# Attention and a token-mixing layer on one core: the same operations written in another order

## The chip, the cores and the metric

The kernel runs on one core of a Trainium2 chip. The metric is device microseconds of one execution, from start to end; less is better. The median of three runs of the kernel before is 121.55 us (121.43 to 121.94).

## The reference

Inputs are fp32; the output is fp32 of 8 x 576 x 512. For each of 8 batches and 8 heads, 32 packed queries `p` attend to 576 keys and values, and the 576 queries `q` then attend to the 32 packed results. The heads are joined to `x` of 576 x 512, and a layer without a softmax mixes the tokens:

```
p_packed = softmax(scale * p @ k.T) @ v              # 32 x 64 per head
out      = softmax(scale * q @ p_packed.T) @ p_packed  # 576 x 64 per head
x        = join_heads(out)                             # 576 x 512 per batch
W        = scale2 * (x @ w_q) @ (x @ w_k).T            # 576 x 576
result   = relu(W @ x) @ w_out
```

## The kernel before

The engines are TensorE (PE), VectorE (DVE), ScalarE (ACT), GpSimd (POOL) and SyncE (SP, which issues transfers). The kernel is a set of small named operations for a batch, each of one engine, and a string `SCHEDULE` (lines 10 to 62) that lists them in the order in which they are recorded. The loop at line 789 reads the string and calls each one. Each engine does its instructions in the order of the string; between engines semaphores hold an instruction until its inputs are there and until its buffer is free. So the string sets the order of each engine and, through it, of all work. No other rule plans it.

An item is `name@batch`, and behind it:

- for PE a colon, the PSUM banks (0 to 4) that it writes, and sometimes a letter: `c` writes the work as halves of 64 columns, `f` as 128 columns, `p` in both ways;
- for an eviction out of PSUM the engine that does it: `v` DVE, `s` ACT. `g` is POOL, and `p` behind a store is SP;
- nothing where only one engine does it.

```
    for item in SCHEDULE.split():
        name, rest = item.split("@")
```

The operations of a batch, in the order of their data:

- `LK`, `LQ`, `LV` load k, q and v (0.59 MB each as bf16) with a transfer that POOL issues and that turns fp32 into bf16 on the way. Batch 0 loads q and v in halves (`LQA`, `LVA`, `LQB`, `LVB`), and its k comes in fp32 through SP at the kernel's start and is cast by `cA0` to `cB1`. `cw` and `wo` load the layer's weights, `LP` loads p. Six buffers stand for each of k, q and v.
- `kt`, `qt` transpose k and q on PE (line 262) in three parts, `ke`, `qe` evict them. Batch 0 does this in four parts, `kf`/`kfe` and `qf`/`qfe`. `tp`, `lp` (batch 0) and `tr`, `lq0`, `lq1` (all others, four scalings each) prepare p's transpose.
- `s0` computes the first scores (line 321), `nm0` takes their maximum on DVE (line 335), `ex0`, `ex1` the exponential on ACT (line 344). `xt`/`xe` transpose the result and evict it, `rc1` takes the reciprocal of the sums, `pv` multiplies with v (line 423), `pp0`, `pp1` scale and mask on DVE, `pt`/`pte` transpose again.
- `e0` computes the second scores (line 507). Then `mx0` (maximum, line 523), `sb0` (subtraction, 526), `x0` (exponential on ACT, 533), `sm0` (sum, 537), `rr0` (reciprocal, 540), and three products on POOL, `ml0`, `ml1`, `ml2` (line 561). `at`/`ae` transpose and evict the product.
- `pq`, `wk`, `wkx`, `wq`, `g`, `y` are the layer's small matmuls, with evictions of the same name and an `e` behind; `m0`, `m1`, `m2` mix the tokens (lines 697 and 719), `r..` evict with the relu, `o0` to `o4` multiply with `w_out` (line 737), `oe..` evict, `st` and `sc` store. The last blocks are stored alone, `o2` of batch 7 in two halves (`o2a`, `o2b`).

Batch 0 is done in halves of its heads at many places (`sA`, `sB`, `nmA`, `pvA`, `ptA`, `mxA` and so on). The scores `s` and the second scores `e_ps` share one buffer of three PSUM banks, so `s0` of a batch waits for `sb0` of another and `e0` for `ex0` and `ex1`. All other PE results turn over in five banks.

`wm@n` (line 782) is PE work whose result nobody reads: n pairs of matmuls of 512 columns with the identity matrix. There are 22 pairs, 9 of them ahead of k's first transposes.

Of the kernel before, what the change touches and what calls it, by code (L numbers as in the profile page):

```python
# [7 lines left out]


SCHEDULE = """  # L10
    wm@8:4 LP@0 LQA@0 LVA@0 cA0@0s cA1@0v LQB@0 wm@1:4 pc@0v kf1@0:2 LVB@0 tp@0:0 kf0@0:4
# [29 lines left out]
    kt1@7:0 ke0@7s qt2@5:2 g@3:1f ke2@7s ke1@7v o3@2:4f sm0@4 ex1@6 pv@5:30 ex0@6 ge@3v
    rr0@4 qe2@5s s0@7 pp1@5 ml0@4g pp0@5 oe3@2s y@3:0 xt1@6:2f nm0@7 pt@5:1f xe1@6s ml2@4g
    xt0@6:4f at0@4:3f ml1@4g ye@3s o2@2:2f ae0@4v ex1@7 pte@5v at1@4:0f xe0@6v oe2@2s
    m2@3:1f ae1@4v qt0@6:4 ex0@7 rc1@6 st1@2 pq@4:3 qt2@6:0 qe0@6v qt0@7:2 pqe@4s st1@1
    qe2@6v e0@5:c r2@3s st0@2 qe0@7s wk@4:0f mx0@5 st0@1 xt0@7:4c wke@4s m1@3:23 o4@3:1f
    r11@3s wkx@4 r10@3s sb0@5 g@4:3f pv@6:02 ge@4s oe4@3s xe0@7v qt1@6:1 pp1@6 y@4:4 wq@4:3
    pp0@6 qe1@6s qt2@7:2 ye@4v xt1@7:0c x0@5 qe2@7v pt@6:4c o2@3:1f pte@6v xe1@7v wqe@4s
    sm0@5 o3@3:4f oe2@3s qt1@7:0 oe3@3s e0@6:p rr0@5 qe1@7v ml0@5g st1@3 m0@4:41 rc1@7 mx0@6
    pv@7:23 r01@4s ml2@5g r00@4s m0@3:10 ml1@5g pp1@7 o1@4:4c r01@3s pp0@7 r00@3s sb0@6
    pq@5:0 at0@5:2c pqe@5s at1@5:3c ae0@5s pt@7:1c o0@3:0c ae1@5v x0@6 pte@7v wk@5:2p  # L50
    o1@3:3c wkx@5 oe1@4s sm0@6 wke@5s m1@4:41 oe1@3s e0@7:p r11@4s wq@5:3 rr0@6 oe0@3s mx0@7
    g@5:2c ml0@6g r10@4s o0@4:1c st0@3 ge@5s wqe@5s st2@3 y@5:2 ml2@6g o3@4:0c sb0@7 ml1@6g
    ye@5s oe0@4s pq@6:2 at0@6:3c oe3@4s m2@5:4c pqe@6v st0@4 at1@6:1c x0@7 ae0@6v m0@5:20
    ae1@6v o2@4:3c r00@5v r2@5s sm0@7 wk@6:1p r01@5s o4@5:2c oe2@4s wq@6:0 wke@6v st1@4
    oe4@5s wkx@6 m1@5:43 rr0@7 g@6:1c st2@5 r10@5s r11@5v o0@5:2c ml2@7g ge@6s wqe@6v ml1@7g
    o3@5:1c oe0@5v ml0@7g at1@7:0c y@6:4 pq@7:3 o2@5:2c ye@6s pqe@7v oe3@5s ae1@7v at0@7:4c
    m0@6:31 ae0@7s o1@5:0c r00@6v oe2@5s r01@6v wk@7:3p st1@5 oe1@5s m1@6:24 wkx@7 o0@6:1c
    r10@6v st0@5 wke@7s r11@6s g@7:3c oe0@6s o1@6:2c ge@7v y@7:3 wq@7:0 oe1@6s o2@6:1c ye@7s
# [770 lines left out]
```

## Time and profile before

| | us |
|---|---|
| median of three runs | 121.55 (121.43 to 121.94) |
| the profiled execution | 122.1 |
| its span in the profile | 120.3 |
| PE busy | 109.1 |
| DVE busy | 99.4 |
| ACT busy | 86.8 |
| POOL busy | 44.7 |

The profile is of one execution. Its page gives the busy time of each engine over the span, the same in forty slices of 3 us, the chain of work that ended last, and groups of instructions by line. Times are from the start of the span. A matmul's end is modelled, so PE's busy time holds short waits. The trace also gives instructions in order of time; counted along the schedule, they give each operation its start.

The loads are one stream: from 5.4 us to 83.9 us the queue that carries them has no gap longer than 0.3 us.

### The profile page before, as it was taken

The numbers are of one execution on the slowest core, as the hardware profiler recorded it, in microseconds if no ns is written. First come the engines' busy times: TensorE is split into PE (matmuls) and PEld (weight loads), VectorE is DVE, ScalarE is ACT, GpSimd is POOL, SyncE is SP. The second block draws the span as 40 slices with busy tenths as digits, with TensorE's granted clock in tenths as the row PEclk, the third lists the DMA queues.
The fourth block names the chain that finished last, engine by engine and source line by source line (L and its number), as shares of the span: only waits on it lengthen the run. The fifth ranks groups of instructions, "written<-read, shape, count | busy, mean of one in ns | idle before, by whom it ended". The sixth has DMA issues, their size and how long they took to land.

```text
span 120.3 us, 4812 instructions
## 1 busy us (share of the span) xinstructions
PE 109.1 (91%) x2121; PEld 76.5 (64%) x2121; DVE 99.4 (83%) x176; ACT 86.8 (72%) x169; POOL 44.7 (37%) x70
## 2 busy tenths in 40 slices
PE   5999786588999999999999999999999999999950
...
DVE  3278799968999979999999999989998999566330
...
GB/s 70 375 165 195 207 208 190 207 208 206 211 205 212 204 209 208 206 208 207 208 226 306 290 209 208 209 255 398 225 180 1 106 335 197 70 230 267 185 291 171
DMA packets 18165, 25.47 MB, mean 212 GB/s; under 512 B 2272, under 2 KB 14816, under 8 KB 18144
## 3 DMA queue, kind: packets, MB, share of 16 engines
...
## 4 chain that ended last, share of the span: by engine, by line
PE 70%; DVE 19%; POOL 2%; ACT 2%; issue 2%; POOLq 0%; DVEq 0%
PE o_ps L737 24%; PE tp_h L262 9%; PE warm L787 6%; PE pv L423 4%; PE m_ps L697 4%; PE tp_a L582 3%; DVE rs L537 3%; PE e_ps L507 3%; PE wq_ps L642 3%; PE tp_x L399 2%; POOL a L561 2%; PE s L321 2%; DVE e L526 2%; DVE mx L523 2%; PE wk_ps L619 2%
## 5 line engine op out<-in xcount | busy, mean ns | idle before, releaser
L561 POOL TENSOR_TENSOR a<-e,rr 128x512 bf16<-128x512 f32 (+1 forms) x24 | 19.3, 828 | 50.4 <-DVE rr L540 45.1
L737 PE MATMUL o_ps<-w_out,reluT 128*64 128x512 bf16 (+2 forms) x236 | 32.3, 373 | 0.1
L737 PEld LDWEIGHTS <-reluT 128*64 128x64 bf16 (+1 forms) x236 | 13.8, 108 | 9.6 <-issue 1.0
L143 ACT ACTIVATE o_sb<-o_ps 128x512 f32<-128x512 f32 x25 | 14.9, 602 | 3.7 <-PE o_ps L737 3.2
L143 ACT ACTIVATE kT<-tp_h 128x768 bf16<-128x768 bf16 (+2 forms) x13 | 9.8, 794 | 5.7 <-PE tp_h L262 5.6
L143 ACT ACTIVATE reluT<-m_ps 128x512 bf16<-128x512 f32 x20 | 11.5, 600 | 2.5 <-PE m_ps L697 2.2
L344 ACT ACTIVATE e1T<-s,nmax 128x576 bf16<-128x576 f32 x16 | 11.8, 755 | 0.6 <-DVE nmax L338 0.5
L262 PE MATMUL tp_h<-ident,q_sb 128*64 128x128 bf16 x288 | 11.9, 221 | 0.2 <-ACT pqk L143 0.2
L533 ACT ACTIVATE e<-e 128x1152 f32<-128x1152 f32 (+2 forms) x9 | 9.5, 1059 | 3.3 <-DVE e L526 3.3
L262 PEld LDWEIGHTS <-q_sb 128*64 128x64 bf16 x288 | 9.8, 110 | 2.8 <-issue 1.7
L523 DVE TENSOR_REDUCE mx<-e_ps 128x36 f32<-128x1152 f32 (+2 forms) x9 | 10.9, 1208 | 0.7 <-PE e_ps L507 0.4
L262 PE MATMUL tp_h<-ident,k_sb 128*64 128x128 bf16 x288 | 11.3, 226 | 0.0
L526 DVE TENSOR_TENSOR e<-e_ps,mx 128x1152 f32<-128x1152 f32 (+2 forms) x9 | 11.0, 1221 | 0.3
L537 DVE TENSOR_REDUCE rs<-e 128x36 f32<-128x1152 f32 (+2 forms) x9 | 10.9, 1211 | 0.2 <-ACT e L533 0.2
L262 PEld LDWEIGHTS <-k_sb 128*64 128x64 bf16 x288 | 9.7, 114 | 1.0 <-issue 0.2
L787 PE MATMUL warm<-ident 128*64 128x512 bf16 x44 | 8.4, 488 | 1.5 <-POOL ident masks.py:199 1.4
L335 DVE TENSOR_REDUCE nmax<-s 128x2 f32<-128x1152 f32 x7 | 9.3, 1327 | 0.0
L145 DVE TENSOR_SCALAR reluT<-m_ps 128x512 bf16<-128x512 f32 x12 | 8.1, 679 | 1.3 <-PE m_ps L697 1.3
L149 DVE COPY qT<-tp_h 128x768 bf16<-128x768 bf16 (+2 forms) x16 | 8.4, 533 | 0.8 <-PE tp_h L262 0.4
L423 PE MATMUL pv<-v_sb,e 64*128 64x256 bf16 x126 | 8.1, 270 | 0.0
L582 PE MATMUL tp_a<-ident,a 128*64 128x128 bf16 (+1 forms) x113 | 6.4, 221 | 1.7 <-POOL a L561 1.7
L143 ACT ACTIVATE qT<-tp_h 128x768 bf16<-128x768 bf16 (+1 forms) x9 | 7.1, 798 | 0.9 <-PE tp_h L262 0.7
...
## 6 DMA issues: line engine op xcount, KB each, us to landing
...
```

The lines of the kernel that those rows point to most:

```text
L143: nc.scalar.activation(dst, src, func, scale=scale)
L262: nc.tensor.transpose(dst[64 * g2:64 * g2 + 64], src[:, g2], ident)
L344: nc.scalar.activation(tile("e1T", [P, NJ, 2, 64], bf16, b)[:, :, h2], S_[b]["s1"][0][h2].rearrange("r (j s) -> r j s", j=NJ), EXP, bias=S ...
L423: nc.tensor.matmul(ps[h2], S_[b]["e1"][r, j, :], S_[b]["v_sb"][r, :, j, :].rearrange("s (g gp) d -> s gp g d", gp=2), start=(j == 0), stop ...
L523: nc.vector.tensor_reduce(tile("mx", [P, NU, 1], fp32, b)[:, r], S_[b]["e"][:, r], axis=AX, op=MAX)
L526: nc.vector.tensor_tensor(tile("e2", [P, NU, L], fp32, b)[:, r], S_[b]["e"][:, r], S_[b]["mx"][:, r].to_broadcast((P, nu, L)), op=SUB,)
L533: nc.scalar.activation(e, e, EXP, scale=scale)
L537: nc.vector.tensor_reduce(tile("rs", [P, NU, 1], fp32, b)[:, r], src[:, r], axis=AX, op=ADD)
L561: (nc.gpsimd if on == "g" else nc.vector).tensor_tensor(tile("a2", [P, NU, L], bf16, b)[:, r], S_[b]["e2"][:, r], S_[b]["rr"][:, r].to_bro ...
L582: nc.tensor.transpose(tp[r, k - k0], a2(b, k % 4 if k < 8 else 4, k // 4)[:, r], ident)
L737: nc.tensor.matmul(ps[r], src[:, i, o:o + P][:, r], w_out[:, i, cols], start=(i == 0), stop=(i == 3),)
L787: nc.tensor.matmul(ps[r], ident[:, r], moving, start=True, stop=True)
```

## The change

Only `SCHEDULE` changes. Every operation stays except the unread pairs, 23 instead of 22: `wm@2:2 wm@1:2 wm@10:4` at the head, so 13 stand ahead of k's first transposes (`kf1`, `kf0`) and 10 of them write one bank in a row. The other 10 stand later.

- 45 evictions and casts go from ACT to DVE and 43 from DVE to ACT; one store goes from SP to ACT and one back. The second part of k's cast (`cA0`) goes to DVE, behind `pc`; `lq1` goes to ACT, behind `ex1@0`; all relu evictions of `m0` and `m1` of batch 0 go to ACT.
- The letters of PE's operations change: 75 have the letter `c` instead of 61, 17 have `f` instead of 33, 11 have `p` instead of 9.
- The order of q's and v's loads at the head stays as it was, `LQA`, `LVA`, `LQB`, `LVB`. On POOL, `LK@3` goes ahead of `ml0@0`, `wo0` goes between `ml1@0` and `ml2@0`, `LQ@5` goes behind `ml1@2`, `LK@7` and `LV@5` go behind `ml0@3`, `LV@6` goes ahead of `LQ@7`, and `LV@7` goes behind `ml2@4`.
- DVE's order from `mx0` of batch 2 to that of batch 3 was mx0@2, ye@1, ke0@4, sb0@2, r01@1, pp0@3, pp1@3, nm0@4, qe0@3, sm0@2, qe1@3, pte@3, rr0@2, r11@1, ke0@6, mx0@3. It is now mx0@2, ke0@4, sb0@2, r00@1, pp1@3, pp0@3, nm0@4, qe2@3, qe0@3, qe1@3, sm0@2, rr0@2, mx0@3.
- The last PE operations were o1, o0, o2b, o2a of batch 7 and are now o2a, o0, o1, o2b. ACT ended with the evictions oe1, oe0 and the stores sc0, sc2b; it now ends with oe0, oe1, sc1, sc2b.

The diff, cut:

```diff
-    wm@8:4 LP@0 LQA@0 LVA@0 cA0@0s cA1@0v LQB@0 wm@1:4 pc@0v kf1@0:2 LVB@0 tp@0:0 kf0@0:4
-    lp@0v LK@1 wm@3:3 kfe0@0s kfe1@0v wm@2:3 cB1@0v LK@2 cB0@0v sA@0 wm@1:3 cw3@0 nmA@0
-    kf3@0:1 kf2@0:3 kfe3@0s cw0@0 tr@0:42 kfe2@0v ex0@0 wm@2:3 lq1@0v lq0@0s sB@0 cw2@0
-    wm@1:3 xa0@0:3 nmB@0 xa1@0:0 xea0@0s qf0@0:2 rcA@0 xea1@0v ex1@0 qf1@0:1 cw1@0 qfe0@0v
-    pvA@0:0 qfe1@0s xb0@0:4 pp0@0 xb1@0:2 xeb0@0s LQ@1 rcB@0 xeb1@0v ptA@0:1f qf3@0:3
-    pteA@0s qfe3@0v e0A@0 wm@4:1 mxA@0 sbA@0 pvB@0:0 LV@1 qf2@0:2 xA@0 pp1@0 qfe2@0v
-    ptB@0:4c smA@0 pteB@0s e0B@0 rrA@0 mxB@0 ml0@0g kt2@1:3 kt1@1:1 sbB@0 ke2@1s kt0@1:0
-    LK@3 at0@0:4c ke0@1v xB@0 ke1@1v ae0@0s smB@0 s0@1 kt0@2:4 rrB@0 nm0@1 kt2@2:1 ml2@0g
-    kt1@2:0 ke2@2s ml1@0g pq@0:2 ke1@2v pqe@0s wo0@0 ex1@1 at1@0:1c ae1@0v wo1@0 ex0@1
-    ke0@2v wq@0:1 LQ@2 wk@0:2p wqe@0s LV@2 s0@2 wkx@0 qt0@1:4 wke@0s LK@4 nm0@2 xt0@1:3f
...
-    pt@1:0c xe0@2v pte@1s m1@0:23 xe1@2v e0@1:c r10@0s LK@6 rc1@2 r11@0v kt1@3:4 mx0@1
-    kt0@3:0 ke1@3s kt2@3:1 LK@5 ke2@3s pq@1:4 sb0@1 o1@0:3c pqe@1s LQ@4 o2@0:4c ke0@3v x0@1
-    oe1@0v s0@3 oe2@0s o0@0:3c sm0@1 qt0@2:4 oe0@0s qt1@2:0 rr0@1 qt2@2:1 qe1@2s nm0@3
-    o3@0:3c ml0@1g qe0@2s ml2@1g oe3@0v at0@1:2f ex1@3 ml1@1g pv@2:40 ae0@1v ex0@3 qe2@2v
-    LV@4 at1@1:2c pp0@2 xt0@3:1f ae1@1s pp1@2 LQ@5 xt1@3:3f rc1@3 xe0@3v pt@2:0c wk@1:2c
-    pte@2s e0@2:f wkx@1 LK@7 wke@1s kt0@4:4 xe1@3s mx0@2 g@1:1c wq@1:0 ge@1s y@1:2 wqe@1s
-    kt1@4:3 ye@1v kt2@4:1 ke0@4v ke1@4s pv@3:02 sb0@2 LV@5 ke2@4s m0@1:43 m2@1:1c r00@1s
-    r01@1v s0@4 x0@2 pp0@3 o0@1:3c pp1@3 nm0@4 r2@1s qt2@3:2 pq@2:0 qt0@3:4 qe2@3s o1@1:1c
-    qe0@3v pqe@2s sm0@2 oe0@1s o4@1:2c oe1@1s qt1@3:0 ex1@4 pt@3:3c qe1@3v kt2@6:1 ex0@4
-    pte@3v m1@1:40 rr0@2 kt0@6:3 r10@1s r11@1v e0@3:c ml1@2g ke2@6s ke0@6v o3@1:0f mx0@3
...
-    st2@1 qt0@4:4 xe1@4v s0@5 wkx@2 qe0@4s st0@0 sm0@3 wq@2:0 wke@2s kt1@6:2 st1@0 wqe@2s
-    qt2@4:4 pv@4:13 qe2@4s rr0@3 nm0@5 ml0@3g pq@3:4 g@2:0c pqe@3s LQ@7 pp1@4 ge@2s qt1@4:4
-    ex1@5 pp0@4 y@2:3 ml1@3g ke1@6v pt@4:1f ye@2s at0@3:0f qe1@4v pte@4s m0@2:32 ex0@5
...
-    mx0@4 at1@3:0f xt0@5:1f ae1@3s o1@2:2f xe1@5s sb0@4 qt0@5:0 xe0@5s wq@3:3 oe1@2s o0@2:1c
...
-    r00@7v r01@7s st1@6 o3@7:1c oe4@7s o1@7:2c st2@7 oe3@7v o0@7:0c oe1@7s sc3@7p o2b@7:3c
-    sc1@7p oe0@7s o2a@7:2c oe2b@7v sc0@7s oe2a@7v sc2b@7s sc2a@7p
+    wm@2:2 wm@1:2 wm@10:4 LP@0 LQA@0 LVA@0 cA1@0v LQB@0 pc@0v cA0@0v LVB@0 tp@0:2 LK@1
+    kf1@0:3 lp@0v kf0@0:4 kfe1@0s wm@3:0 LK@2 kfe0@0v cB1@0s cB0@0v sA@0 cw0@0 wm@2:1 nmA@0
+    kf3@0:3 kf2@0:0 kfe3@0v tr@0:24 ex0@0 cw2@0 kfe2@0v sB@0 lq0@0s wm@1:0 nmB@0 cw3@0
+    xa0@0:0 xa1@0:1 rcA@0 qf0@0:3 xea0@0s xea1@0v qf1@0:2 ex1@0 qfe0@0v pvA@0:1 cw1@0
+    qfe1@0v lq1@0s pp0@0 xb0@0:0 xb1@0:2 xeb0@0v ptA@0:1f xeb1@0v qf2@0:0 LQ@1 pteA@0v e0A@0
+    qfe2@0v wm@4:2 mxA@0 rcB@0 sbA@0 pvB@0:0 xA@0 LV@1 qf3@0:1 pp1@0 qfe3@0v ptB@0:0c smA@0
+    pteB@0s e0B@0 rrA@0 mxB@0 kt0@1:3 LK@3 kt1@1:4 sbB@0 ke0@1s kt2@1:1 ml0@0g ke1@1v xB@0
+    ke2@1v at0@0:4c smB@0 s0@1 ae0@0s kt1@2:2 rrB@0 nm0@1 kt2@2:0 ml1@0g kt0@2:4 ke2@2s
+    pq@0:1 wo0@0 ke0@2v ex1@1 ke1@2v ml2@0g ex0@1 wo1@0 at1@0:2c LQ@2 ae1@0v pqe@0s s0@2
...
+    y@0:0 xt0@2:1c pp1@1 ye@0s qe1@1v xe0@2s pt@1:2c xt1@2:4c rc1@2 pte@1v m1@0:30 xe1@2s
+    e0@1:c LK@6 r10@0s r11@0s m0@0:14 mx0@1 kt1@3:3 r00@0s LK@5 kt2@3:0 r01@0s kt0@3:2
+    ke1@3s sb0@1 o2@0:1c LQ@4 ke0@3s o1@0:3c ke2@3v x0@1 pq@1:4 o0@0:2c pqe@1s sm0@1 oe1@0s
+    s0@3 oe2@0s o3@0:3c oe0@0s rr0@1 nm0@3 qt0@2:4 ml0@1g oe3@0s qt2@2:1 qt1@2:2 qe0@2s
+    ml1@1g qe1@2v at0@1:0f ex1@3 pv@2:34 qe2@2v ae0@1v ex0@3 ml2@1g LV@4 at1@1:2f pp1@2
+    xt0@3:0f pp0@2 ae1@1s xt1@3:1f xe0@3v pt@2:4f xe1@3v wk@1:3p pte@2s rc1@3 kt2@4:0 wke@1v
+    e0@2:c wkx@1 ke2@4s g@1:3f mx0@2 wq@1:4 ge@1s y@1:2 kt0@4:3 wqe@1s kt1@4:1 ke0@4v ye@1s
+    sb0@2 ke1@4s m0@1:34 pv@3:02 r01@1s r00@1v x0@2 m2@1:4c s0@4 pp1@3 o0@1:3c pp0@3 r2@1s
+    nm0@4 pt@3:2c oe0@1s qt2@3:0 qt1@3:4 pte@3s qe2@3v qt0@3:3 ex1@4 o1@1:2c qe0@3v ex0@4
+    qe1@3v m1@1:10 sm0@2 oe1@1s kt0@6:4 e0@3:c ke0@6s o4@1:2f rr0@2 r10@1s mx0@3 ml1@2g
+    r11@1s pq@2:3 kt2@6:1 pqe@2s o3@1:4c ke2@6s LQ@5 sb0@3 xt0@4:3c ml0@2g oe3@1s kt0@5:0
...
+    wk@2:4p qe2@4s rr0@3 pv@4:23 wke@2v ex0@5 ml0@3g rc1@4 qe0@4v ex1@5 wkx@2 wq@2:1 pp1@4
+    LK@7 kt1@6:0 wqe@2s pp0@4 g@2:3c LV@5 ke1@6v at0@3:4c ge@2s pt@4:1c ae0@3v y@2:2 ml1@3g
...
+    r11@2v LQ@6 e0@4:p r00@2s r10@2v at1@3:4c LV@6 r01@2s xt0@5:1f mx0@4 ae1@3s qt0@5:3 LQ@7
...
+    pq@4:1 nm0@7 y@3:4 qe2@5s o2@2:2c ml2@4g LV@7 ye@3s at1@4:3f pqe@4v ex0@7 ml0@4g pt@5:0f
...
+    o1@3:2c sm0@6 wke@5s r11@4s g@5:1c e0@7:p ge@5s rr0@6 oe1@3s pq@6:0 r10@4v y@5:3 o0@4:1c
...
+    o3@6:4c r2@7s st0@6 m1@7:10 o4@7:3f r10@7s r11@7v oe3@6s m0@7:02 oe4@7v o3@7:4c st1@6
+    r00@7s r01@7v st2@7 o2a@7:3c oe3@7v o0@7:0c oe2a@7v sc3@7p o1@7:3c oe0@7s sc2a@7p
+    o2b@7:4c sc0@7p oe1@7s oe2b@7v sc1@7s sc2b@7s
```

More of the change, by code (lines that the diff above doesn't have):

```diff
@@ L17 @@
-    ptB@0:4c smA@0 pteB@0s e0B@0 rrA@0 mxB@0 ml0@0g kt2@1:3 kt1@1:1 sbB@0 ke2@1s kt0@1:0
-    LK@3 at0@0:4c ke0@1v xB@0 ke1@1v ae0@0s smB@0 s0@1 kt0@2:4 rrB@0 nm0@1 kt2@2:1 ml2@0g
-    kt1@2:0 ke2@2s ml1@0g pq@0:2 ke1@2v pqe@0s wo0@0 ex1@1 at1@0:1c ae1@0v wo1@0 ex0@1
-    ke0@2v wq@0:1 LQ@2 wk@0:2p wqe@0s LV@2 s0@2 wkx@0 qt0@1:4 wke@0s LK@4 nm0@2 xt0@1:3f
-    g@0:1f LV@3 qt1@1:0 ge@0s xe0@1s y@0:2 qe1@1v xt1@1:1c ye@0s rc1@1 xe1@1v ex0@2 m0@0:30
-    pv@1:21 r00@0v LQ@3 ex1@2 qe0@1v r01@0s qt2@1:3 pp1@1 xt0@2:4c pp0@1 xt1@2:1c qe2@1v
@@ L29 @@
-    kt1@4:3 ye@1v kt2@4:1 ke0@4v ke1@4s pv@3:02 sb0@2 LV@5 ke2@4s m0@1:43 m2@1:1c r00@1s
-    r01@1v s0@4 x0@2 pp0@3 o0@1:3c pp1@3 nm0@4 r2@1s qt2@3:2 pq@2:0 qt0@3:4 qe2@3s o1@1:1c
-    qe0@3v pqe@2s sm0@2 oe0@1s o4@1:2c oe1@1s qt1@3:0 ex1@4 pt@3:3c qe1@3v kt2@6:1 ex0@4
-    pte@3v m1@1:40 rr0@2 kt0@6:3 r10@1s r11@1v e0@3:c ml1@2g ke2@6s ke0@6v o3@1:0f mx0@3
-    ml2@2g ml0@2g xt0@4:3f oe3@1s kt1@5:4 xe0@4v kt2@5:0 LQ@6 ke1@5s sb0@3 at1@2:3f at0@2:1f
-    ke2@5s o2@1:4f ae1@2v ae0@2s xt1@4:0f rc1@4 oe4@1s oe2@1v kt0@5:3 x0@3 wk@2:1p ke0@5v
@@ L35 @@
-    st2@1 qt0@4:4 xe1@4v s0@5 wkx@2 qe0@4s st0@0 sm0@3 wq@2:0 wke@2s kt1@6:2 st1@0 wqe@2s
-    qt2@4:4 pv@4:13 qe2@4s rr0@3 nm0@5 ml0@3g pq@3:4 g@2:0c pqe@3s LQ@7 pp1@4 ge@2s qt1@4:4
-    ex1@5 pp0@4 y@2:3 ml1@3g ke1@6v pt@4:1f ye@2s at0@3:0f qe1@4v pte@4s m0@2:32 ex0@5
-    ae0@3v ml2@3g m1@2:14 r00@2v LV@6 qt1@5:0 r01@2s e0@4:p qe1@5v LV@7 r10@2s xt1@5:3f
-    mx0@4 at1@3:0f xt0@5:1f ae1@3s o1@2:2f xe1@5s sb0@4 qt0@5:0 xe0@5s wq@3:3 oe1@2s o0@2:1c
-    rc1@5 r11@2v wqe@3s qe0@5v wk@3:2p x0@4 s0@6 wkx@3 wke@3v kt0@7:4 oe0@2s nm0@6 kt2@7:3
@@ L41 @@
[L41 to L58, printed above, removed]
@@ L59 @@
-    wqe@7v st0@6 m2@7:4c oe2@6v m1@7:02 o3@6:3c r11@7s r2@7v r10@7s m0@7:42 oe3@6s o4@7:0c
-    r00@7v r01@7s st1@6 o3@7:1c oe4@7s o1@7:2c st2@7 oe3@7v o0@7:0c oe1@7s sc3@7p o2b@7:3c
-    sc1@7p oe0@7s o2a@7:2c oe2b@7v sc0@7s oe2a@7v sc2b@7s sc2a@7p
+    wm@2:2 wm@1:2 wm@10:4 LP@0 LQA@0 LVA@0 cA1@0v LQB@0 pc@0v cA0@0v LVB@0 tp@0:2 LK@1
+    kf1@0:3 lp@0v kf0@0:4 kfe1@0s wm@3:0 LK@2 kfe0@0v cB1@0s cB0@0v sA@0 cw0@0 wm@2:1 nmA@0
+    kf3@0:3 kf2@0:0 kfe3@0v tr@0:24 ex0@0 cw2@0 kfe2@0v sB@0 lq0@0s wm@1:0 nmB@0 cw3@0
@@ new lines @@
+    rc1@1 LV@2 xt1@1:3c nm0@2 wk@0:2p xt0@1:0c LK@4 qt0@1:4 xe0@1s qt2@1:1 LV@3 wkx@0 qe0@1s
+    wke@0v wq@0:0 xe1@1v ex0@2 qe2@1v g@0:3f ge@0v ex1@2 pv@1:42 wqe@0v LQ@3 qt1@1:3 pp0@1
+    y@0:0 xt0@2:1c pp1@1 ye@0s qe1@1v xe0@2s pt@1:2c xt1@2:4c rc1@2 pte@1v m1@0:30 xe1@2s
+    e0@1:c LK@6 r10@0s r11@0s m0@0:14 mx0@1 kt1@3:3 r00@0s LK@5 kt2@3:0 r01@0s kt0@3:2
+    ke1@3s sb0@1 o2@0:1c LQ@4 ke0@3s o1@0:3c ke2@3v x0@1 pq@1:4 o0@0:2c pqe@1s sm0@1 oe1@0s
+    s0@3 oe2@0s o3@0:3c oe0@0s rr0@1 nm0@3 qt0@2:4 ml0@1g oe3@0s qt2@2:1 qt1@2:2 qe0@2s
@@ new lines @@
+    r11@1s pq@2:3 kt2@6:1 pqe@2s o3@1:4c ke2@6s LQ@5 sb0@3 xt0@4:3c ml0@2g oe3@1s kt0@5:0
+    kt1@5:1 xe0@4v kt2@5:4 x0@3 ml2@2g ke1@5v o2@1:3f ke0@5v oe4@1s ke2@5v at1@2:1f xt1@4:0c
+    sm0@3 ae1@2s st2@1 at0@2:4c s0@5 xe1@4s qt2@4:1 ae0@2s st1@0 nm0@5 qt0@4:0 oe2@1s st0@0
+    wk@2:4p qe2@4s rr0@3 pv@4:23 wke@2v ex0@5 ml0@3g rc1@4 qe0@4v ex1@5 wkx@2 wq@2:1 pp1@4
+    LK@7 kt1@6:0 wqe@2s pp0@4 g@2:3c LV@5 ke1@6v at0@3:4c ge@2s pt@4:1c ae0@3v y@2:2 ml1@3g
+    qt1@4:0 pte@4s pq@3:3 ye@2s qt1@5:4 qe1@4v pqe@3s m1@2:21 qe1@5s rc1@5 ml2@3g m0@2:30
@@ new lines @@
+    r11@2v LQ@6 e0@4:p r00@2s r10@2v at1@3:4c LV@6 r01@2s xt0@5:1f mx0@4 ae1@3s qt0@5:3 LQ@7
+    o0@2:2c xe0@5s sb0@4 o1@2:1c oe0@2s qe0@5s xt1@5:0c wk@3:4p xe1@5v x0@4 s0@6 wkx@3
+    wke@3v kt1@7:2 nm0@6 oe1@2s wq@3:4 ke1@7s kt2@7:0 kt0@7:1 ke2@7v o3@2:3c ex1@6 ke0@7v
+    ex0@6 sm0@4 g@3:1f pv@5:02 ge@3s oe3@2s wqe@3s rr0@4 s0@7 pp0@5 ml1@4g pp1@5 qt2@5:3
+    pq@4:1 nm0@7 y@3:4 qe2@5s o2@2:2c ml2@4g LV@7 ye@3s at1@4:3f pqe@4v ex0@7 ml0@4g pt@5:0f
+    oe2@2v xt0@6:1f qt0@6:4 ex1@7 rc1@6 pte@5v st1@2 xt1@6:2c xe0@6v m2@3:0c xe1@6s st1@1
```

14 lines of the change are left out of this document (added).

## The prediction

> **What bounds the kernel now.** I read the page first, then the busy time in stretches, then the chain of waits, then the instructions in order of time. Page, parts 1 and 2:
>
> ```profile
> span 120.3 us, 4812 instructions
> PE 109.1 (91%) x2121; PEld 76.5 (64%) x2121; DVE 99.4 (83%) x176; ACT 86.8 (72%) x169; POOL 44.7 (37%) x70
> PE   5999786588999999999999999999999999999950
> DVE  3278799968999979999999999989998999566330
> ```
>
> Each digit is 3 us. PE has holes only at the start, between 12 and 25 us, and at the end. DVE is full from 24 to 99 us. The stretches say it sharper (length, then busy us of PE, PEld, DVE, ACT, POOL):
>
> ```profile
> 15.00:20.00 5.00, 4.01 (x107) 2.87 (x99) 4.70 (x10) 1.72 (x3) 1.61 (x2) 1.00 1.37 198
> 20.00:25.00 5.00, 2.69 (x66) 2.07 (x67) 4.51 (x9) 3.35 (x7) 3.32 (x6) 1.00 1.26 206
> ...
> 45.00:50.00 5.00, 5.00 (x104) 4.13 (x104) 5.00 (x8) 4.62 (x8) 0.00 (x0) 1.00 1.21 208
> ...
> 70.00:75.00 5.00, 5.00 (x99) 3.58 (x96) 5.00 (x10) 4.88 (x10) 0.84 (x1) 1.00 1.21 208
> ...
> 105.00:110.00 5.00, 5.00 (x92) 3.05 (x90) 3.03 (x7) 3.26 (x7) 0.00 (x0) 1.00 0.54 208
> ```
>
> So there are three stages: up to about 44 us batch 0's and 1's softmax chains on DVE set the pace and PE waits; from 44 to 95 us PE and DVE are both full; after 95 us only PE is. The change is one of order, so the question is which engine finds its next input late.
>
> **The change, part by part.** The sum is made on the profiled execution, 122.1 us (span 120.3, 1.8 around it); the median of the runs shown is 121.55, so I take 0.55 off at the end.
>
> *Work.* The groups by line, shapes apart, give prices: DVE kT copy 0.55, reluT 0.68, o_sb 0.69, maximum 1.34, subtraction 1.35; ACT 0.82, 0.60, 0.60 for the first three. 45 operations go from ACT to DVE and 43 the other way; adding the rows, DVE has 106.95 us before and 106.90 after, ACT 99.35 and 98.80. PE has one more unread pair. More work is written in halves of 64 columns, 76 more matmuls, but in the chain five tp_x of 128 columns take 0.28 us and ten of 64 take 0.28: nothing. What moves is when.
>
> *A: the head.* The chain, with start and length:
>
> ```profile
> 1.37 3.64 PE warm L787 x16
> 5.06 0.64 PE warm L787 x2
> 5.70 0.43 PE tp_h L262 x8
> 6.23 0.53 PE tp_h L262 x10
> 6.76 0.73 PE warm L787 x6
> ...
> 10.08 0.68 DVE pT_bd L147 x2
> ...
> 10.79 0.69 DVE pT_bd L147 x2
> 11.51 0.76 DVE nmax L338
> ```
>
> The unread pairs start 0.43 us apart at first, at 15.17 us eight matmuls (four pairs) take 0.86, 0.215 a pair; a pair of transposes takes 0.107 here and 0.057 later (12 in 0.34). So PE runs at half rate until about 6.8 us. After the change 13 pairs stand ahead of k's transposes instead of 9. Two, then one in the same bank: the weight load at 5.06 waited 0.52 where its neighbours waited 0.25, so a reused bank costs 0.27. Ten follow in another bank: 1.37 + 2 x 0.43 + 0.27 + 0.43 = 2.9, nine at half rate to 6.8, one at 0.22: 7.05. The transposes then run at full rate (0.06 + 0.22 + 0.28, to 7.6), kfe0 takes 0.49 on DVE from 7.85, and sA starts at 8.45 against 7.97: +0.45 at the first maximum. The cast of k's second part goes to DVE behind pc and is ready by 5.9, under the unread block.
>
> Most of it comes back. In the fence, lq1 (1.4 us, four scalings) stands on DVE ahead of the second maximum. After the change ACT does it, behind ex1. DVE gets kfe3 (0.43) there and the four unread matmuls ahead of sB are gone: second maximum at 11.1 instead of 11.51. ACT's lq0 waits for tr and ends later, xea0 at 12.4 instead of 11.8, so pvA starts at 12.5 instead of 12.58 and pp0 at 13.2 instead of 13.37. Between pp0 and mxA DVE then has xeb0, pteA and another q copy, 2.13 us instead of 1.59: mxA 15.4 (15.21), mxB 19.0 (18.88). A is **+0.1**, the late start hidden by the freed DVE; without that cover it would be +0.45.
>
> *B: batch 1 to mx0@2.* DVE's work between mx0@1 and mx0@2 is 10.57 both ways. POOL now issues wo0 (0.64) between ml1 and ml2, so at1@0 starts near 24.75 (24.07); DVE does ke1@2 meanwhile. wkx and wke of batch 0 come after nm0@2, a microsecond later, but pv@1 comes earlier, and mx0@1 falls at 32.9 (33.01). Then ACT has xe0, xe1 and all four r of batch 0 (3.7 us by rows) ahead of ke1@3, ke0@3 and x0@1: x0@1 36.0 (35.78), and o1@0 and o3@0 wait on PE for their banks (ke1@3 and oe1@0, about 0.5 us each). I get mx0@2 at 44.5 against 44.08: **+0.4**, A included. Bounds: -0.2 if ACT never waits, +0.8 with every wait in full.
>
> *C: the full stretch.*
>
> ```profile
> 44.08 1.36 DVE L523 TENSOR_REDUCE mx<-e_ps 128x36 f32<-128x1152 f32 x1 [0.29 <-PE e_ps L494]
> ...
> 93.90 1.30 DVE L523 TENSOR_REDUCE mx<-e_ps 128x36 f32<-128x1152 f32 x1
> ```
>
> From mx0@2 to mx0@7 DVE took 49.8 us for rows that add to 52.94 (they overlap a little): 0.94. After the change they add to 53.54: 0.6 x 0.94 = **+0.55**, mx0@7 at +0.95. It is spread otherwise: mx0@2 to mx0@3 falls from 11.02 to 9.51 (ye, r11, pte and ke0@6 leave, qe2 joins), the rest rises from 41.92 to 44.03. PE's rows after e0@7 fall from 22.88 to 22.15, since more output projection stands ahead; that stage is PE's alone, so **-0.73** comes off. PE ends at +0.95 - 0.73 = +0.2. The bounds of a stall in between: PE's idle time from 25 to 115 us sums to 1.4 us, which is all that it can win; a PE that waits another 1.5 us is no more than the hole at 20 to 25 has.
>
> *D: the end.*
>
> ```profile
> 115.24 0.60 ACT L143 ACTIVATE o_sb<-o_ps 128x512 f32<-128x512 f32 x1 [0.22 <-PE o_ps L737]
> 115.67 0.86 DVE L149 COPY o_sb<-o_ps 128x256 f32<-128x256 f32 x2 [1.05 <-PE o_ps L737]
> 115.86 1.32 ACTq L764 DMA_DIRECT2D out_dram<-o_sb  x2
> ```
>
> PE ends at 116.07; ACT's last eviction was of a block that PE finished 0.87 us earlier. After the change o1, which ends 0.43 before PE does, is evicted by ACT (0.60), which then issues two stores (0.66 each), the last of them the last half block's: from PE's end -0.25 + 0.60 + 1.32 = 1.67 us instead of 117.18 - 116.07 = 1.11, with a landing of 2.4 to 3.0 us in both: **+0.45** (0 if SP's store lands last anyway, +0.6 in full).
>
> *Loads.* On POOL, LQ@5 now stands behind ml1@2 and LK@7, LV@5 behind ml0@3, which started at 61.96; before they were issued at 42 to 44. The trace's landings put v@4 at 58.3, q@5 at 61.2, k@7 at 65.1, v@5 at 71.3, and pv@5 at 72.8. A load issued to an idle queue moves its first packet 2.2 us later (p_b: 3.16, 5.4), so the load stream stands still from 61.2 to about 64. SP's stores of batches 0 and 1, issued from 58.4, then took the DMA time that put 6.2 us instead of 2.8 between k@7 and v@5. I let them fill the hole: cost 0, v@5 near 70.
>
> Sum: 0.2 + 0.45 = +0.65: 122.75 on the profiled execution, **122.2** on the median; 121.5 to 123.0 with these bounds.
>
> The Trainium skill ("TensorE: Matmul & The Clock Gate", Part 1) says the full clock comes after a busy window of about 3.4 us whose phase is not tied to the kernel's start. The trace agrees as far as it goes: matmuls for 3.6 us from 1.37 did not bring it, and it came 5.4 us after the first. By that rule an execution could get it anywhere from 4.8 to 8.2 us, which is the third rival below.
>
> **Rivals.** *1, faster.* DVE has 2.1 us less ahead of mx0@3 and about 2 less ahead of rr0@4 and mx0@5. If B's waits on ACT do not happen, the stretch moves up until PE's own 1.4 us of idle time are used; with the end's +0.45: -0.95, **120.6**. For it: DVE has no gap in 45 to 50. Against: the two engines are full together, and the work is given back by mx0@7.
>
> *2, slower by the loads.* If the stores do not fill the hole at 61 to 64 us, v@5 lands 2.8 us later, 74.1, and pv@5, due about 73.0, holds PE 1.1 us, and more where q@6 follows: 122.2 + 1.3 = **123.5**. It decides from the point where more than 1.7 us of the hole stay empty. For it: v@5 has only 1.5 us in hand now. Against: k@7 and q@6 have more.
>
> *3, the unread block does not do what its name says.* Full rate from 4.8 us would end the block at 6.0 instead of 7.05 and start sA a microsecond earlier; the chain through the maxima hands on perhaps 0.7: **121.5**, no change. For it: nothing but the trace's one phase fixes 6.8. Against: before has the same freedom.
>
> **How the numbers follow.** Forecast 0.45, faster 0.25, loads 0.15, block 0.15. A measurement of this kernel tells about 0.5% (0.6 us) from no change, so slower means above 122.15 and faster below 120.95. The forecast gives slower 0.32, same 0.13; the first rival faster 0.22, same 0.03; the second slower 0.15; the third same 0.12, faster 0.03. Sum: faster 0.25, same 0.28, slower 0.47. The range reaches to both ends, 120.6 and 123.5.
>
> **What would show it.** A: k's first transposes near 7.0 us, the second maximum near 11.1. B: mx0@2 at 44.5, x0@1 late, PE waiting for ke1@3's bank. C: mx0@7 near 94.9. D: ACT's two stores last, ending 1.6 us behind PE. Loads: a hole at 61 to 64 us with stores in it. I am wrong if mx0@3 comes a microsecond or more early and PE keeps it, or if PE waits for pv@5.

## The result, and the profile after

The changed kernel takes 122.36 us (median of 20 runs, 121.85 to 124.45) against 121.73 of the kernel before in the same session (20 runs, 121.25 to 122.33): ratio 1.0057, 95% interval 1.0033 to 1.0082. It is slower by 0.6%, as forecast (122.2). Executions more than 1.5% above the fastest of the same kernel are left out of every ratio: one here, one to four in e0 to e3 and e11, none of the kernel before.

The profiled execution does not show it: 122.0 us, span 120.2, against 122.1 and 120.3 before. So the first question was why its profile is not slower, and the second where the loss is. Page, parts 1 and 2 of the changed kernel:

```profile
span 120.2 us, 4965 instructions
...
PE 107.5 (89%) x2197; PEld 75.2 (63%) x2197; DVE 98.5 (82%) x175; ACT 86.8 (72%) x170; POOL 44.8 (37%) x70
...
PE   5999775599999989999997999999999999999950
...
DVE  3377899889679899999989699999799997785910
```

DVE's row had nothing below an 8 from 45 to 102 us before. Now it has a 6 (66 to 69 us), a 7 (84 to 87) and another 7 at 99. The same five stretches as before (length, then busy us of PE, PEld, DVE, ACT, POOL):

```profile
15.00:20.00 5.00, 2.93 (x88) 2.48 (x87) 4.80 (x12) 2.09 (x4) 2.34 (x3) 1.00 1.38 197
20.00:25.00 5.00, 3.27 (x78) 2.53 (x79) 4.22 (x9) 3.60 (x8) 3.28 (x5) 1.00 1.24 209
45.00:50.00 5.00, 5.00 (x98) 3.70 (x98) 4.99 (x8) 4.64 (x9) 0.00 (x0) 1.00 1.21 208
70.00:75.00 5.00, 4.96 (x93) 3.27 (x87) 4.97 (x8) 4.37 (x10) 1.67 (x3) 1.00 1.21 206
105.00:110.00 5.00, 5.00 (x92) 3.17 (x90) 3.60 (x7) 2.37 (x6) 0.00 (x0) 1.00 0.85 292
```

The three stages are still there. The head, in order of time, changed kernel:

```profile
1.37 5.16 PE L787 MATMUL warm<-ident 128*64 128x512 bf16 x26 [1.37 <-POOL ident masks.py:199]
...
10.38 0.76 DVE L338 TENSOR_REDUCE nmax<-s 128x1 f32<-128x576 f32 x1 [0.74 <-PE s L321]
```

The 13 unread pairs end at 6.53, where I expected 7.05, and the second maximum starts at 10.38 (before 11.51, expected 11.1). A second profile of the same kernel (e0 below) has another head:

```profile
1.37 6.03 PE L787 MATMUL warm<-ident 128*64 128x512 bf16 x26 [1.37 <-POOL ident masks.py:199]
...
11.30 0.76 DVE L338 TENSOR_REDUCE nmax<-s 128x1 f32<-128x576 f32 x1 [0.74 <-PE s L321]
```

The same 26 matmuls take 5.16 us in the one and 6.03 in the other, and all that follows is 0.92 later. The trace's record of the granted clock says why: its entry of full clock begins at 5.51 us in the one, at 7.33 in the other. (The PEclk column shows 1.00 before that too, since there is no entry.) The matmuls agree: the unread pairs start about 0.42 us apart up to 5.4 us in the one and up to 6.7 in the other, and about 0.21 apart from 5.7 and, where the next ones stand, from 7.8. In the profile of before the entry begins at 6.78. With a second profile of before (e8) and one hybrid (e10), in us:

| | before | before, again | change | change, again | change up to mx0@2 (e10) |
|---|---|---|---|---|---|
| full clock from | 6.78 | 6.12 | 5.51 | 7.33 | 5.71 |
| first scores (sA) | 7.97 | 7.65 | 7.67 | 8.58 | 7.78 |
| mx0@1 | 33.01 | 32.69 | 31.76 | 32.69 | 32.57 |
| mx0@2 | 44.08 | 43.77 | 43.02 | 43.94 | 43.82 |
| mx0@2 to mx0@7 | 49.82 | 49.82 | 51.51 | 51.65 | 49.90 |
| mx0@7 to PE's end | 22.17 | 22.17 | 21.19 | 21.20 | 22.17 |
| PE's end to span's end | 4.26 | 4.24 | 4.50 | 4.49 | 4.13 |
| span | 120.3 | 120.0 | 120.2 | 121.3 | 120.0 |

In both kernels a clock that comes 1 us later moves everything behind the head by half a microsecond (0.92 for 1.82, 0.31 for 0.66). Brought to before's 6.78, the two profiles of the change have mx0@2 at 43.66, 0.42 earlier than before. The slope is drawn through these two; e4 and e6 below, with the same order up to mx0@2, give 43.64 by it, and e3 43.91, which stays open. Then the change loses 1.69 and 1.83 up to mx0@7, wins 0.98 behind it, and loses 0.24 at the end. The sum, with the first of the two, is -0.42 + 1.69 - 0.98 + 0.24 = **+0.53**, near the medians' +0.63. The profile of the change looked no slower because its clock came 1.27 us earlier than before's: 0.64 us, a loan of that one execution.

The loss is the stretch from mx0@2 to mx0@7. One window over it, kernel before, then changed:

```profile
44.08:93.90 49.82, 49.45 (x1034) 36.19 (x1030) 48.12 (x80) 44.58 (x86) 13.42 (x17) 1.00 1.02 219
```

```profile
43.02:94.53 51.51, 49.96 (x1124) 36.27 (x1124) 48.75 (x79) 45.64 (x89) 15.33 (x20) 1.00 1.02 215
```

DVE is busy 0.63 us longer (48.75 - 48.12; I had 0.55) and idle 2.76 us instead of 1.70. This second part, 1.06, is what the prediction did not have. DVE's two longest waits in this stretch, changed kernel:

```profile
68.16 0.42 DVE L149 COPY e<-tp_x 128x512 bf16<-128x512 bf16 x1 [0.97 <-PE tp_x L399]
...
85.58 0.29 DVE L149 CAST g<-g_ps 128x128 bf16<-128x128 f32 x1 [0.67 <-PE g_ps L667]
```

Both waits are for PE, and ahead of both PE itself stood in the middle of an operation. The releaser named is "issue": the profile shows nothing that PE waited for.

```profile
64.29 0.40 PE L399 MATMUL tp_x<-ident,e1T 128*128 128x128 bf16 x4
65.48 0.23 PE L399 MATMUL tp_x<-ident,e1T 128*128 128x128 bf16 x1 [0.80 <-issue]
...
84.61 0.62 PE L737 MATMUL o_ps<-w_out,reluT 128*64 128x512 bf16 x4 [0.21 <-issue]
```

The first wait of DVE follows from the first stall; in e3 below, without that stall, DVE does not stand here. Of the second, 0.33 us are the second stall: in e0, e2 and e3 below, where PE does not stand there, DVE waits 0.33 to 0.34 us for the same operation. So the new idle time of this profile, 1.06 us, is 0.97 + 0.33 from the two stalls, less 0.24 elsewhere.

At the same time ACT stands for a transfer. In this profile that costs nothing more: it ends at 86.01, after DVE's wait, and PE has no idle time behind it. Changed kernel:

```profile
86.01 0.60 ACT L143 ACTIVATE o_sb<-o_ps 128x512 f32<-128x512 f32 x1 [1.62 <-DMA out_dram<-o_sb]
86.51 0.38 ACT L143 ACTIVATE y<-y_ps 128x256 bf16<-128x256 f32 x1
```

The first eviction is oe2 of batch 3. Its staging buffer `o_sb1` has two copies, so it needs the one that batch 1 filled, and `st1@1` must have left it. The stores issued between 76 and 88 us take 9.1 us to land (median of five; 7.2 before), beside the loads of batches 6 and 7: the landing times put v@7 at 87.16 (before 84.2), and pv@7 starts at 87.20, the moment that v@7 is there. Before, it had 3.2 us in hand (2.0 to 2.3 in e8, e9 and e10).

This landing is a floor under the stalls. From the start of pv@7 to mx0@7 it is 7.32 or 7.33 us in all eight profiles that have the change's order there, and 6.53 or 6.54 in the six that have before's. So in the change's order mx0@7 comes no earlier than 7.3 us behind v@7's landing, and without PE's stalls pv@7 would have waited for v@7, as it does in e2 and e3 (0.62 and 1.18 us).

The end, changed kernel:

```profile
115.32 0.60 ACT L143 ACTIVATE o_sb<-o_ps 128x512 f32<-128x512 f32 x1 [0.27 <-PE o_ps L737]
...
115.95 1.30 ACTq L764 DMA_DIRECT2D out_dram<-o_sb  x2
```

PE ends at 115.72; ACT's second issue ends at 117.25, 1.53 behind it (expected 1.67).

### The profile page after: what moved, and what is told of

Its sections match the earlier page's. It is cut to its first block, busy times and chain, and to the rows that moved or that the text cites. A ratio compares the mean times of both kernels' runs of the same rounds, so it can differ in the third digit from the quotient of the medians.

```text
span 120.2 us, 4965 instructions
## 1 busy us (share of the span) xinstructions
PE 107.5 (89%) x2197; PEld 75.2 (63%) x2197; DVE 98.5 (82%) x175; ACT 86.8 (72%) x170; POOL 44.8 (37%) x70
## 4 chain that ended last, share of the span: by engine, by line
PE 53%; DVE 23%; ACT 7%; issue 3%; POOL 1%; DVEq 0%; POOLq 0%
PE o_ps L737 20%; PE tp_h L262 6%; PE pv L423 4%; DVE rs L537 4%; PE m_ps L697 3%; DVE e L526 3%; DVE mx L523 3%; PE tp_a L582 3%; PE e_ps L507 3%; DVE nmax L335 3%; PE s L321 2%; DVE kT L149 2%; PE wq_ps L642 2%; ACT kT L143 2%; DVE pp L439 2%
## 5 line engine op out<-in xcount | busy, mean ns | idle before, releaser
L737 PE MATMUL o_ps<-w_out,reluT 128*64 128x512 bf16 (+1 forms) x260 | 32.3, 374 | 0.3 <-issue 0.2
L737 PEld LDWEIGHTS <-reluT 128*64 128x64 bf16 x260 | 14.0, 110 | 9.4 <-issue 1.5
L143 ACT ACTIVATE o_sb<-o_ps 128x512 f32<-128x512 f32 x21 | 12.3, 598 | 5.8 <-PE o_ps L737 4.1
L143 ACT ACTIVATE reluT<-m_ps 128x512 bf16<-128x512 f32 x25 | 13.9, 598 | 2.5 <-PE m_ps L697 2.2
L143 ACT ACTIVATE kT<-tp_h 128x768 bf16<-128x768 bf16 (+1 forms) x10 | 7.8, 797 | 7.2 <-PE tp_h L262 7.1
L262 PE MATMUL tp_h<-ident,q_sb 128*64 128x128 bf16 x288 | 11.2, 220 | 0.1
L262 PE MATMUL tp_h<-ident,k_sb 128*64 128x128 bf16 x288 | 10.3, 219 | 0.0
L262 PEld LDWEIGHTS <-k_sb 128*64 128x64 bf16 x288 | 9.0, 110 | 1.3 <-issue 0.5
L149 DVE COPY o_sb<-o_ps 128x512 f32<-128x512 f32 (+1 forms) x12 | 7.4, 639 | 2.0 <-PE o_ps L737 2.0
L582 PEld LDWEIGHTS <-a 128*64 128x64 bf16 (+1 forms) x125 | 5.0, 108 | 5.0 <-POOL a L561 3.5
```

The source lines that it names most:

```text
L143: nc.scalar.activation(dst, src, func, scale=scale)
L149: nc.vector.tensor_copy(dst, src)
L262: nc.tensor.transpose(dst[64 * g2:64 * g2 + 64], src[:, g2], ident)
L582: nc.tensor.transpose(tp[r, k - k0], a2(b, k % 4 if k < 8 else 4, k // 4)[:, r], ident)
L737: nc.tensor.matmul(ps[r], src[:, i, o:o + P][:, r], w_out[:, i, cols], start=(i == 0), stop=(i == 3),)
```

## The experiments

Twelve kernels ran, four at a time beside the kernel before. The first four asked whether the clock, the halves, the head or the end makes the difference; the next four turned on the loads, which every profile of the first four showed late; the last four cut the change along its order.

**e0**, the changed kernel again.

> The changed kernel as it is, timed again beside before on the same chip as the next three. Steady-order theory (the forecast): 1.005 of before in every execution, the loss spread over DVE's heavier second half and the end. Clock theory: its executions differ by when PE gets its full rate; those that get it early (about 5.5 us, as in the profiled one) take about 122.0, those that get it near 7 us or later 123 and more, while before's stay within half a microsecond. Fetch theory: a stall of about 1 us in the middle of xt0 of batch 5, with no operand late, comes back in any new profile.

Measured: 123.28 us (121.82 to 125.49, 12 runs), ratio 1.0077 (1.0041 to 1.0112). The clock's start moves the head as in the table; of the 1.06 us between the two profiled executions (123.06, 122.0) the clock makes 0.92. But it is not the whole spread: the kernel before has the same freedom of the clock, and its executions spread over 1.1 to 1.2 us; those in the change's two ratios spread over 1.7. PE's first stall is there again, the second not. ACT's wait is there again, and here it costs: y@4 stands behind it, PE's m0@4 behind y (0.77 us), and pv@7 starts 0.50 us after v@7 has landed:

```profile
87.12 0.60 ACT L143 ACTIVATE o_sb<-o_ps 128x512 f32<-128x512 f32 x1 [2.01 <-DMA out_dram<-o_sb]
87.61 0.38 ACT L143 ACTIVATE y<-y_ps 128x256 bf16<-128x256 f32 x1
```

**e1**, 21 operations of PE whole instead of in halves.

```diff
-xt0@1:0c
-e0@2:c
-o3@1:4c
+xt0@1:0f
+e0@2:f
+o3@1:4f
...
```

> 21 of PE's operations written as 128 columns again, as before has them; order, engines and banks stay. Fetch theory (PE runs out of instructions because halves double their number): the stall of 1.07 us at 65.5 us in xt0 of batch 5 goes and the one of 0.3 to 0.5 at 84.6 in o3 of batch 3 too, 0.6 to 1.2 us faster than the changed kernel. Steady-order theory: the letters cost nothing, the time stays within 0.2 us of the changed kernel, and the hole at 65.5 stays or moves to the next operation.

Measured: 123.19 us (122.34 to 124.77), ratio 1.0101 (1.0062 to 1.0141): not faster. The stall at 65.5 is gone from its profile, and PE comes to v@5 before v@5 does. PE's row, e1:

```profile
72.28 1.16 PE L423 MATMUL pv<-v_sb,e 64*128 64x256 bf16 x18 [0.58 <-DMA v_sb<-in_v_dram]
```

So these 21 halves cost nothing that the time shows, and where the stall goes a transfer is late next.

**e2**, nine unread pairs ahead of k's transposes instead of 13.

```diff
-wm@2:2 wm@1:2 wm@10:4 LP@0
-cA1@0v LQB@0 pc@0v
+wm@8:4 LP@0
+cA1@0v LQB@0 wm@1:4 pc@0v
```

> Nine unread pairs ahead of k's transposes instead of 13 (eight and one, as before has them); all else of the changed kernel stays. Clock theory: the block of 13 costs most where the full rate comes late, so the spread of the executions shrinks to about 0.7 us and the median falls by 0.3 to 0.5 us. Steady-order theory: the head is hidden by DVE's freed work, within 0.15 us of the changed kernel.

Measured: 122.50 us, ratio 1.0044 (1.0018 to 1.0070), which the change's interval holds. With the clock from 5.36, sA starts at 7.44; the change with the clock from 5.51 has 7.67. So the four pairs make sA about 0.15 us later at the same clock. Whether that reaches mx0@2 this profile does not tell (43.44 against 43.02), since PE stood 0.49 us ahead of 29.62, again with "issue". Neither of the stalls in the change's profile is there, and pv@7 waits for v@7:

```profile
87.31 1.16 PE L423 MATMUL pv<-v_sb,e 64*128 64x256 bf16 x18 [0.62 <-DMA v_sb<-in_v_dram]
```

**e3**, the last store on SP.

```diff
-oe2b@7v sc1@7s sc2b@7s
+oe2b@7v sc1@7s sc2b@7p
```

> Only the last half block's store goes from ACT's queue to SP's. If the end costs what the forecast says (ACT issues two stores of 0.65 us after its last eviction), 0.3 to 0.45 us faster than the changed kernel. If the last landing is set by something else, no change.

Measured: its times (median 124.16, 121.83 to 125.30, 6 runs) give no ratio; only the profile is read. From PE's end to the span's end it has 4.3 us instead of 4.5. The end costs 0.2 by ACT's second issue. PE's instructions are those of the change, and here tp_x runs through, while the transfers are later still:

```profile
64.45 0.45 PE L399 MATMUL tp_x<-ident,e1T 128*128 128x128 bf16 x5
```

```profile
87.87 1.16 PE L423 MATMUL pv<-v_sb,e 64*128 64x256 bf16 x18 [1.18 <-DMA v_sb<-in_v_dram]
```

**e4**, the loads LQ@5, LK@7, LV@5 early again.

```diff
-ml2@1g LV@4 at1@1:2f
+ml2@1g LV@4 LQ@5 LK@7 LV@5 at1@1:2f
...
```

> The changed kernel with LQ@5, LK@7 and LV@5 issued by POOL right behind LV@4, as early as in the kernel before; nothing else moved. Theory 1 (the late loads leave v@7 no time in hand, so every variation of the transfers lengthens an execution): no hole in the load stream at 61 to 62 us, v@7 lands near 84 us instead of 87.2 to 87.8, pv@7 doesn't wait, the median falls by 0.5 us or more against the changed kernel, to 121.4 to 121.9 (ratio to the kernel before 0.996 to 1.001), and the spread of the times shrinks from 2.5 us to about 1. Theory 2 (the order of the steady stretch and the end cost the 0.6%, the loads only look late): v@7 lands earlier, but the ratio stays at 1.004 to 1.008 and the spread where it was.

Measured: 123.26 us (122.40 to 124.23), ratio 1.0123 (1.0081 to 1.0165): not faster than the change, and by the medians slower, where I expected 0.5 faster. The loads did what was meant: no hole, v@7 at 85.6, pv@7 at 88.78 with 3.2 us in hand. But ACT now stands 20 us earlier, PE waits 0.30 and 0.95 us for ACT behind that, and PE's first stall is there too (0.98 us):

```profile
69.34 0.60 ACT L143 ACTIVATE o_sb<-o_ps 128x512 f32<-128x512 f32 x1 [2.19 <-DMA out_dram<-o_sb]
```

The eviction is oe0@2, which needs the buffer of st0@0. The change issues st1@0 ahead of st0@0 (before: st0@0 first). With the hole, the two land at 63.0 and 65.4, and oe0@2 runs at 67.07 without a wait for them; with loads in the hole they land at 67.2 and 69.3. So the change's late loads and its order of stores belong together: undoing the loads alone brought no gain here. (Early loads with st0@0 first were not tried.)

**e5**, the kernel before with the change's load order.

```diff
-ml0@3g pq@3:4
+ml0@3g LK@7 LV@5 pq@3:4
-xe1@6s ml2@4g xt0@6:4f
+xe1@6s ml2@4g LV@7 xt0@6:4f
...
```

LQ@5, LQ@6, LQ@7 and LV@6 move as well. (The change moves LQ@6 too, behind ml2@3.)

> The kernel before with the change's load order alone: LQ@5 behind ml1@2, LK@7 and LV@5 behind ml0@3, LQ@6, LQ@7 and LV@6 behind ml2@3, LV@7 behind ml2@4. Theory 1 (late loads): a hole of 1 to 2 us in the load stream near 61 us, v@7 lands 86.5 us or later, pv@7 (due 87.4 here) starts when it lands, ratio 1.003 to 1.008, spread up to 2.5 us. Theory 2 (the order of the steady stretch and the end): the same landings, but ratio 0.998 to 1.002 and a spread of about 1 us.

Measured: 122.91 us (122.47 to 123.58), ratio 1.0098 (1.0066 to 1.0129): slower, as the first theory said, but not where it said. v@7 lands at 87.55 and pv@7 starts at 88.41, without a wait. POOL, then DVE:

```profile
74.29 1.40 POOL L561 TENSOR_TENSOR a<-e,rr 128x512 bf16<-128x512 f32 x2 [6.39 <-PE pv L423]
75.64 0.81 POOL L153 DMA_DIRECT2D v_sb<-in_v_dram  x1
76.47 1.06 POOL L561 TENSOR_TENSOR a<-e,rr 128x512 bf16<-128x512 f32 x1
```

```profile
78.08 0.49 DVE L149 COPY a2T<-tp_a 128x640 bf16<-128x640 bf16 x1 [0.68 <-PE tp_a L582]
```

The issue of LV@7, 0.81 us of POOL, stands ahead of the last product of batch 4, and at0@4 waits for that: mx0@5 is at 80.17 instead of 79.28. The run tells that late loads cost this order 0.9 us up to mx0@5, by the place of one issue on POOL, and leaves open what the landing alone would cost.

**e6**, the early loads and the last store on SP.

> The early loads of the run before last, and the last store (sc2b of batch 7) issued by SP instead of ACT. If the end costs what the prediction's term D says (ACT's second issue of 0.66 us stands behind the last half block's eviction), 0.3 to 0.45 us below the kernel with early loads alone (ratio to the kernel before 0.993 to 0.998). If the store of SP lands last anyway, within 0.15 us of it.

Measured: 123.43 us, ratio 1.0119 (1.0083 to 1.0155), not told apart from e4 by the times. By the profiles, PE ends at 117.3 in both, and the span ends at 121.6 instead of 121.8: again 0.2.

**e7**, the early loads and the 21 whole operations.

> The early loads, and 21 operations of PE that the change writes in halves of 64 columns written whole, as before. If the extra matmuls cost time by themselves, or by PE's instruction fetches (stalls of about 1 us in the middle of an operation in two of four profiles so far), 0.4 us or more below the kernel with early loads alone. If halves cost nothing, as predicted, within 0.25 us of it.

Measured: 123.42 us (122.98 to 124.49), ratio 1.0144 (1.0108 to 1.0181), not faster than e4. The stall at 66 us is gone here too, and ACT waits for st0@0 until 68.82 all the same.

**e8**, the kernel before again.

> The kernel before, unchanged, for a second profile of it. If the start of the full clock moves the head and nothing else, sA and mx0 of batches 1 and 2 start half a microsecond later per microsecond that the clock comes later than 6.78 us (as the changed kernel's did: mx0@1 31.76, 32.29, 32.69 with the clock at 5.51, 6.59, 7.33), and mx0@2 to mx0@7 takes 49.8 again. If before's 49.8 was a lucky execution, 50.5 or more. Ratio 0.999 to 1.001.

Measured: 121.77 us, ratio 0.9992 (0.9966 to 1.0017); mx0@2 to mx0@7 in 49.82 again, to 0.01. The stretch of before did not vary between the two profiles. Its spread of 1.1 us is what clock starts from 5.3 to 7.7 us (those of all fourteen profiles) would make at half a microsecond each, by an estimate: 1.2.

**e9**, the change's order up to mx0@1, before's from there.

> The changed order up to mx0 of batch 1, then all that is left in the order, with the letters and banks, of the kernel before (loads of batches 5 to 7, stores and the end too). Theory 3 (at the same clock start the change gains about 0.6 us up to mx0@1 and 0.4 up to mx0@2, and loses it between mx0@2 and mx0@7 and at the end): mx0@1 near 32.4 with the clock at 6.8, mx0@2 to mx0@7 in 49.8 to 50.2, ratio 0.995 to 0.998. Theory 4 (the change's head and batch 1 are worth nothing, since the full stretch takes the same time from wherever it starts): ratio 0.999 to 1.002.

Measured: 122.16 us (121.76 to 122.61), ratio 1.0030 (1.0008 to 1.0051). Outside the expectation: mx0@1 is 0.6 early for its clock (32.04 with 6.06), but mx0@2 comes 12.13 us later (before 11.07), so the seam between the two orders loses more than the head has won. Then the stretch takes 49.83.

**e10**, the same with the cut at mx0@2.

> The same with the cut at mx0 of batch 2. Theory 3: mx0@2 near 43.65 with the clock at 6.8 (before 44.08), mx0@2 to mx0@7 in 49.8 to 50.3, ratio 0.996 to 0.999. Theory 4: ratio 0.999 to 1.002. If it is 1.004 or more, as the whole change, the loss is ahead of mx0@2 after all.

Measured: 121.55 us (121.03 to 121.98, 12 runs) against 121.81, ratio 0.9977 (0.9953 to 1.0001). The stretch, e10:

```profile
43.82:93.72 49.90, 49.14 (x1013) 36.01 (x1013) 48.19 (x80) 43.54 (x84) 13.43 (x17) 1.00 1.02 219
```

It is 0.26 us below the kernel before in the same session, but the interval just reaches 1; its spread is 0.95 us. So what the change does ahead of mx0@2 loses nothing and may win a quarter of a microsecond, which is not clear of the noise. The loss of the whole change, which is clear of it (1.0033 to 1.0082), lies behind mx0@2: 0.6 to 0.9 us by the medians. The profile does not show the gain: mx0@2 is at 43.82 with the clock from 5.71, that is 44.36 at 6.78, where I expected 43.65. PE stood in the middle of unread work ahead of 15.60 here, which cost 0.7 us up to mx0@1.

**e11**, the same with the cut at mx0@3.

> The same with the cut at mx0 of batch 3, which the change reaches 1.7 us earlier at the same clock start, with ten operations still to do that the kernel before had behind it. Theory 3: mx0@3 near 52.55 with the clock at 6.8; the work that is owed (DVE's ke, r11 and casts, some 1.5 us of rows) is given back by mx0@7; ratio 0.994 to 1.0. If the loss sits in the change's order from mx0@2 to mx0@3, ratio 1.004 or more.

Measured: 123.42 us, ratio 1.0107 (1.0064 to 1.0149). It says little about the change: mx0@3 is early as expected (52.98 with the clock from 7.65), but at the seam pq@2 waits 1.36 us for a reluT, DVE then 2.17 for tp_x, and mx0@4 comes 14.5 us later.

## Why the prediction was right, and where it was not

The sign and the size came out (122.2 forecast, 122.36 measured), but the size is luck: two errors of about a microsecond, -0.8 and +1.1, cancel in it. Terms by the table, at before's clock start:

| term | forecast | measured |
|---|---|---|
| A and B, to mx0@2 | +0.4 | -0.42 |
| C, mx0@2 to mx0@7 | +0.55 | +1.69 |
| C, PE behind mx0@7 | -0.73 | -0.98 |
| D, the end | +0.45 | +0.24 |
| sum | +0.67 (rounded there to 0.65) | +0.53 |

**A** was right in mechanism: sA at 8.31 for the same clock (forecast 8.45), the second maximum at 11.02 (11.1), so the freed DVE does hide the late start. mxB is at 18.6 (19.0).

**B** failed in sign. I charged about 0.5 us each for o1@0 and o3@0 waiting on their banks; PE's idle time from 33 to 38.8 us sums to 0.24, 0.18 of it behind POOL, and x0@1 is at 35.2 (36.0), behind the four relu evictions that were to hold it. The lower bound of -0.2 would have been nearer.

**C** was right where it added rows: DVE's busy time grew by 0.63, and mx0@2 to mx0@3 takes 8.9 us (9.51 x 0.94 = 8.94). It failed where it said that a stall of PE is worth at most what the hole at 20 to 25 is, and put nothing in for one: DVE has 1.06 us of new idle time.

**Loads: cost 0** is the step that failed. The hole was there (60.8 to 62.3 us) and the stores of batches 0 and 1 landed in it, as I said; v@5 came at 71.4, and pv@5 did not wait. What I did not follow was the end of the stream: what is issued late ends late, v@7 by 2 to 3 us, and the second set of stores falls into its last transfers. The second rival had the mechanism and the wrong place: not v@5 at 74, but v@7 at 87 and, in e0, the buffer of st1@1.

An estimate of the size from the traces: up to pv@7 the change takes 44.18 us from mx0@2 (before 43.29), and behind it 7.33 (6.53). Without the waits for v@7, pv@7 would stand 43.25 us behind mx0@2 in e2 and 43.51 in e3. So of the 1.69 us some 0.8 to 1.0 belong to the order itself, where I had 0.55, and 0.7 to 0.9 to the late transfers, where I had 0.

No run shows this alone: e4 gave the loads back and lost more through st0@0, and e5 moved an issue on POOL with them. What e4, e5 and e10 suggest together is that each of the two orders has its loads and stores fitted to each other; the traces show that before's has 2 to 3 us in hand at v@7, and the change's none.

**PE's stall without a missing operand** is what DVE waited for in the change's profile (0.97 us, and 0.33 at the second), 0.75 us in e0's, and nothing in e3's with the same instructions. But e3 did not come to mx0@7 sooner: where the stall is gone, PE waits for v@7 instead (DVE waits 1.85 us for pv@7). So in these profiles the stalls stand in time that the late transfers would have cost anyway. They would add to the time where v@7 is early, as in e4. The wider spread of the change, 1.7 us against 0.85 to 1.2 of the orders that have before's stretch whole (before, e8, e9, e10), fits waits that vary with the transfers; that is argued, not shown.

**D** was right in mechanism and too large: 0.24, of which ACT's second issue is 0.2 (e3, e6).

**The halves** cost nothing, as said: e1 and e7 are not faster than their partners.

**The first rival** saw that mx0@3 would come early; it does, by 1.7 us at the same clock. What the prediction held against it came true as well: the work is given back by mx0@7. From mx0@3 to mx0@4 the change takes 0.9 us longer, from mx0@5 to mx0@7 2.1 us, and of these DVE is busy for 1.8. **The third rival** took the clock for a property of the change. It is one of the execution: the full clock began between 5.3 and 7.7 us in the fourteen profiles. That agrees with the Trainium skill ("TensorE: Matmul & The Clock Gate", Part 1) as far as it goes, inside the 4.8 to 8.2 that the prediction estimated from it.
